# Retention, ELU and maxout layers on one core: the first block from the first chunk of every batch, without a state

## The chip, the cores and the metric

One core of a Trainium2 chip runs the whole program in one launch. The metric is device time in microseconds (us), the median of several executions. TensorE is called PE, VectorE DVE, ScalarE ACT, GpSimd POOL and the engine that issues most DMAs SP.

## The reference

Three layers in a row: a linear attention with a decaying state, a dense layer with an ELU, and a maxout layer.

```python
# q, k, v: (4 batches, 8 heads, 768 steps, 64)
for t in range(S):
    state = gamma[None, :, None, None] * state + np.einsum('bhd,bhe->bhde', k[:, :, t], v[:, :, t])
    y[:, :, t] = scale * np.einsum('bhd,bhde->bhe', q[:, :, t], state)
# x: (3072 tokens, 512)
h = x @ w_in                                    # 512 x 2048
g = np.where(h > 0.0, h, np.exp(np.minimum(h, 0.0)) - 1.0)
x = g @ w_out                                   # 2048 x 512
h = np.maximum(np.maximum(x @ w1, x @ w2), x @ w3)   # 512 x 768 each
return h @ w_out2                               # 768 x 512
```

The state runs through the 768 steps of one batch and starts anew in the next. The matrices w_in to w_out2 are given as 64-bit floats.

## The kernel before

**Attention by chunks.** The 768 steps of a batch are cut into 6 chunks of 128 steps, 24 in all, numbered batch after batch. A chunk needs its own scores (queries times keys, masked by decays), times its values, plus the decayed queries times the state of all earlier chunks; and it hands on state = decay x state + keys times values. Four chunks (CB) make a block of 512 tokens, six blocks in all. Chunks 0 to 3 go through the `wide_` functions, all 128 steps at once; each of them waits for the state of the one before. The later ones go through `scores`, `mask`, `update`, `carry`, `values`, `finish`, in two halves of 64 steps, with `middle` as the state between the halves; `visit(c)` closes chunk c and opens the next. `keys_of` and `queries_of` make the decayed keys (kd) and queries (qd) on POOL. `state` is a pair of tiles that take turns.

**Dense layer by blocks.** For block b and hidden tile f (16 of 128 units), `h1(b, f)` is x @ w_in as 12 products of 512 columns (L400), then the ELU: exp and relu on ACT (L407, L408), max on DVE (L411), the high part gh on ACT (L412) and the low part gl on DVE (L415). `o1(b, f, ...)` adds g @ w_out into four banks of PSUM, again 12 products (L434). Each operand is split into a high and a low half of reduced precision, three products for one. `x2_out` takes the four banks to `x2d` in DRAM.

**Weights.** The 64-bit words of w_in and w_out are loaded in 32 halves of 512 KB (`load_half`, L333; half 2f holds w_in's tile f, 2f + 1 w_out's) and turned into high and low parts: `cv_bits` on ACT (L342), `cv_rest` on DVE (three instructions, L349 to L355), `cv_high` on ACT (L365), `cv_low` on DVE (L370). `cv_rest(n)` also issues half n + 2, since two buffers take turns.

**Order.** All engines run in the order in which the program is written. Until all halves are converted, blocks 0 and 1 go in turns in seven groups of f, so that one new f comes with one or two products that need none. When a group ends its partial sums leave PSUM, and are added to the older ones on DVE (L451); two of the older sums wait in SBUF, the others are stored to `x2d` and loaded again (`renew`):

```python
groups = [(0, 0, 2), (1, 0, 4), (0, 2, 6), (1, 4, 8), (0, 6, 11), (1, 8, KFF), (0, 11, KFF)]
groups += [(b, 0, KFF) for b in range(2, NB)]
seq = [(b, f, f0, f1) for b, f0, f1 in groups for f in range(f0, f1)]
```

In the loop over `seq` step i issues h1 of step i + 1 and then o1 of step i; `third(i)` puts chunks 8 to 12 between them (it opens chunk 8 at i = 23), later blocks carry a chunk at every fourth f. The maxout layer follows from `x2d`. Loads at the start all go through SP's queue: chunk 0, decays, mask, chunks 1 to 3 with halves 0 and 1 between them, chunk 4. A chunk has q and k transposed, by two partition halves of 64 rows, and k and v by token on 128 rows.

Of the kernel before, what the change touches and what calls it, by code (L numbers as in the profile page):

```python
# [42 lines left out]
def kernel(ctx: ExitStack, tc: tile.TileContext, qkv0, qkv, wa, wb, dmask, qdec, cols, out):  # L43
# [33 lines left out]
    def load(c, part=None):  # L77


        if c >= NCHUNK:  # L80
            return

        early = c < EARLY
        src = qkv0 if early else qkv
        if part != 1:
            if c in raw_t:
                return
            if early:
                x = wpool.tile([P, NPAIR, 4, P], F32, tag="w", name="x")
            else:  # L90
                x = ld.tile([P, NPAIR, 4, P], F32, tag="r", name="x")
            raw_t[c] = x
            if early:
                for h, at_, o, n in ((rows(0), 0, 0, 1), (rows(0), 1, 2, 1), (rows(1), 0, 1, 2)):
                    nc.sync.dma_start(
                        out=x[h, :, at_:at_ + n, :].rearrange("d p s t -> d p (s t)"),
                        in_=src[c, :, h, o * P:(o + n) * P].rearrange("p d t -> d p t"),
                    )
            else:
                for g in range(2):  # L100
                    for s in range(2):
                        for p in range(1 if c < 2 * NCH else 2):
                            ps = slice(None) if c < 2 * NCH else slice(p, None, 2)
                            cc = slice((2 * s + (g ^ p)) * P, (2 * s + (g ^ p) + 1) * P)
                            nc.sync.dma_start(
                                out=x[rows(g), ps, s, :], in_=src[c, ps, rows(g), cc].rearrange("p d t -> d p t")
                            )
        if part != 0:
            x = raw_t[c]
            o = 3 * P if early else 4 * P  # L110
            nc.sync.dma_start(
                out=x[:, :, 2:4, :].rearrange("t p s n -> t p (s n)"),
                in_=src[c, :, :, o:].rearrange("p t n -> t p n"),
            )
# [6 lines left out]
    def seat(c, p, r):  # L121
        return r if c < 2 * NCH else r ^ (p & 1)
# [5 lines left out]
    def swap():  # L128
        for g in range(2):
            nc.sync.dma_start(out=qdec_sb[rows(g), 1::2, :], in_=qdec[rows(1 - g), 1::2, :])  # L130
            nc.sync.dma_start(
                out=cols_sb[rows(g), H + 1:H + NPAIR:2], in_=cols[rows(1 - g), H + 1:H + NPAIR:2]
            )

    def later(swapped):
        far = cols_sb[:, H + NPAIR:H + 2 * NPAIR]
        nc.vector.reciprocal(out=far, in_=cols_sb[:, H:H + NPAIR])
        late = qdec_sb[:, 1::2, HC:P] if swapped else qdec_sb[:, :, HC:P]
        by = far[:, 1::2] if swapped else far
        n = NPAIR // 2 if swapped else NPAIR  # L140
        nc.vector.tensor_tensor(out=late, in0=late, in1=by.unsqueeze(2).to_broadcast([P, n, HC]), op=ALU.mult)

    def keys_of(c):
        if c >= NCHUNK:
            return
        kd = at.tile([P, NPAIR, 2, D], F32, tag="kd", name="kd", bufs=2)
        nc.gpsimd.tensor_tensor(  # L147
            out=kd, in0=raw_t[c][:, :, 2, :].rearrange("t p (r d) -> t p r d", r=2),
            in1=cols_sb[:, 0:H].rearrange("t (p r) -> t p r", r=2).unsqueeze(3).to_broadcast([P, NPAIR, 2, D]),
            op=ALU.mult,  # L150
        )
# [22 lines left out]
    def mask(c):  # L174
# [5 lines left out]
        for g in range(2):  # L180
# [3 lines left out]
                in1=d[:, :, g::2, :] if c < 2 * NCH else d[:, :, 0::3, :] if g == 0 else d[:, :, 1:3, :],  # L184
# [5 lines left out]
    def update(c, banks):  # L190
# [3 lines left out]
        kd = st_t[c][1]  # L194
        v = raw_t[c][:, :, 3, :].rearrange("t p (r d) -> t p r d", r=2)
        for p in range(NPAIR):
            for r in range(2):
                for s in range(2):
                    nc.tensor.matmul(  # L199
                        banks[s][rows(seat(c, p, r)), p, :], kd[rows(s), p, r, :], v[rows(s), p, r, :],  # L200
                        start=False, stop=p == NPAIR - 1, skip_group_check=True,
                    )

    def carry(c):
        if c >= NCHUNK:
            return
        new, old, up = state[c % 2], state[1 - c % 2], up_t.pop(c)
        if c % NCH == 0:
            nc.vector.tensor_copy(middle, up[0])
        else:  # L210
            nc.gpsimd.tensor_tensor(
                out=middle, in0=old, in1=cols_sb[:, H:H + NPAIR].unsqueeze(2).to_broadcast([P, NPAIR, D]), op=ALU.mult
            )
            nc.vector.tensor_tensor(out=middle, in0=up[0], in1=middle, op=ALU.add)
        if c % NCH != NCH - 1:
            nc.vector.tensor_tensor(out=new, in0=up[1], in1=middle, op=ALU.add)

    def past(c, cross):
        qd = st_t[c][0]
        for p in range(NPAIR):  # L220
            for g in range(2):
                r, s = seat(c, p, g), g ^ cross
                if c % NCH == 0 and s == 0:
                    continue
                src = middle if s else state[1 - c % 2]
                last = nc.tensor.matmul(  # L226
# [58 lines left out]
    def wide_mix(c):  # L285
        v = raw_t[c][:, :, 3, :].rearrange("t p (r d) -> t p r d", r=2)
        a = a_t.pop(c)
        xo = xo_t[c] = ps_h.tile([P, NPAIR, P], F32, tag="h", name="xo")
        for p in range(NPAIR):
            for r in range(2):  # L290
                nc.tensor.matmul(
                    xo[rows(r), p, :], v[:, p, r, :], a[:, r, p, :],
                    start=p == 0, stop=c == 0 and p == NPAIR - 1,
                )
        if c:
            qd = st_t[c][0]
            for p in range(NPAIR):
                for r in range(2):
                    nc.tensor.matmul(
                        xo[rows(r), p, :], state[1 - c % 2][rows(r), p, :], qd[rows(r), p, :],  # L300
                        start=False, stop=p == NPAIR - 1,
                    )
# [7 lines left out]
    def wide_update(c):  # L310
        kd = st_t.pop(c)[1]
        v = raw_t.pop(c)[:, :, 3, :].rearrange("t p (r d) -> t p r d", r=2)
        up = ps_h.tile([P, NPAIR, D], F32, tag="h", name="up")
        for p in range(NPAIR):
            for r in range(2):
                nc.tensor.matmul(up[rows(r), p, :], kd[:, p, r, :], v[:, p, r, :], start=p == 0, stop=p == NPAIR - 1)
        new, old = state[c % 2], state[1 - c % 2]
        if c == 0:
            nc.vector.tensor_copy(new, up)
        else:  # L320
            nc.vector.tensor_tensor(
                out=new, in0=old, in1=cols_sb[:, H:H + NPAIR].unsqueeze(2).to_broadcast([P, NPAIR, D]), op=ALU.mult
# [866 lines left out]
```

## Time and profile before

| | |
|---|---|
| median of 3 runs | 993.1 us (992.72 to 996.32) |
| the profiled execution | 993.37 us, its span 991.6 us |
| PE busy | 963.9 us, 97% of the span |
| DVE, ACT, POOL busy | 585.1, 343.7, 95.0 us |
| PE's mean granted clock | 0.997 of full speed |
| chain that ended last | PE 83%, DVE 7%, DMA 4%, ACT 3% |

Busy time is of one execution. A line L400 is a line of the kernel above. The chain is followed back from the last instruction to whatever released each step. In a row of time the first number is the start and the second the time covered; PE's products overlap, so their rate is read from one start to the next.

### The profile page before, as it was taken

How to read it: one execution, taken by the hardware profiler on the slowest of the kernel's cores; microseconds unless marked ns; L12 is line 12 of the kernel's file. 1: busy time of each engine (PE TensorE's matmuls, PEld its weight loads, DVE VectorE, ACT ScalarE, POOL GpSimd, SP SyncE). 2: the span in 40 equal slices, each digit the busy share in tenths (PEclk: the TensorE clock that was granted, in tenths of full speed). 3: DMA queues.
4: the chain of work that ended last, by engine and by line, in shares of the span. 5: the costliest groups of instructions: out<-in, count | busy, mean ns of one | idle time of the engine just before them, and what ended most of it. 6: DMA issues, size and time to landing. Idle time of an engine off the chain costs nothing.

```text
span 991.6 us, 16233 instructions
## 1 busy us (share of the span) xinstructions
PE 963.9 (97%) x6644; PEld 785.8 (79%) x6644; DVE 585.1 (59%) x956; ACT 343.7 (35%) x619; POOL 95.0 (10%) x119
## 2 busy tenths in 40 slices
PE   7789999999999999999999999999999999999998
PEld 5667787878888888887888888878888788888886
DVE  2767888753555655666555662477653686436650
ACT  1345554533344444444444553121130212201111
POOL 2310001012111110111110000010100010000100
PEclk9999999999999999999999999999999999999999
DMA  9923345544545555555545444356535556236602
GB/s 225 234 64 105 107 150 185 154 129 113 176 142 160 166 170 165 160 164 168 163 138 170 159 134 164 121 176 204 184 111 202 175 178 199 85 128 208 193 13 85
DMA packets 83721, 151.92 MB, mean 153 GB/s; under 512 B 7232, under 2 KB 58432, under 8 KB 77504
## 3 DMA queue, kind: packets, MB, share of 16 engines
q1 hardware_dynamic: 74000, 94.01, 31.4%
q0 software_dynamic: 7344, 52.69, 16.2%
q10 hardware_dynamic: 2304, 4.20, 1.2%
q8 instruction: 52, 0.85, 0.4%
q14 instruction: 21, 0.17, 0.1%
HBM read 116.53 MB, written 34.34 MB: 152 GB/s over the span
## 4 chain that ended last, share of the span: by engine, by line
PE 83%; DVE 7%; DMA 4%; ACT 3%; issue 1%; POOL 1%; SPq 1%; POOLq 0%; ACTq 0%
PE hp L763 25%; PE acc L434 22%; PE hp L400 22%; PE acc L823 10%; DMA x<-in_qkv 3%; DVE e L411 1%; DVE t L352 1%; PE xs L226 1%; ACT gh L412 1%; PE xs L169 1%; PE xs L239 1%; PE xs L199 1%; DVE w L370 1%; DVE gl L415 1%; DVE t L349 1%
## 5 line engine op out<-in xcount | busy, mean ns | idle before, releaser
L763 PE MATMUL hp<-seat,w 128*128 128x512 f32 x1134 | 259.8, 390 | 3.3 <-DVE m L772 3.3
L763 PEld LDWEIGHTS hp<-seat,w 128*128 128x128 f32 x1134 | 212.1, 188 | 49.7 <-DVE m L772 6.1
L400 PE MATMUL hp<-xh,w 128*128 128x512 f32 x768 | 245.1, 390 | 3.8 <-ACT w L365 2.9
L434 PE MATMUL acc<-gh,w 128*128 128x512 f32 x768 | 205.8, 396 | 4.1 <-ACT gh L412 1.5
L434 PEld LDWEIGHTS acc<-gh,w 128*128 128x128 f32 x768 | 141.8, 188 | 39.1 <-ACT gh L412 3.8
L400 PEld LDWEIGHTS hp<-xh,w 128*128 128x128 f32 x768 | 143.7, 188 | 35.2 <-ACT w L365 4.3
L400 PE MATMUL hp<-xl,w 128*128 128x512 f32 x384 | 141.9, 390 | 0.7 <-DVE xl L261 0.7
L411 DVE SCALAR_TENSOR_TENSOR e<-e,hp 128x512 f32<-128x512 f32 x96 | 65.7, 685 | 124.6 <-ACT e L408 123.7
L434 PE MATMUL acc<-gl,w 128*128 128x512 f32 x384 | 110.7, 390 | 0.0
L407 ACT ACTIVATE e<-hp 128x512 f32<-128x512 f32 x96 | 57.0, 594 | 123.5 <-PE hp L400 121.7
L823 PE MATMUL acc<-w,g 128*128 128x512 f32 x432 | 99.1, 389 | 0.0
L415 DVE TENSOR_TENSOR gl<-e,gh 128x512 fp32r<-128x512 f32 x96 | 66.5, 692 | 52.2 <-ACT gh L412 50.9
L823 PEld LDWEIGHTS acc<-w,g 128*128 128x128 f32 x432 | 81.1, 188 | 16.8
L412 ACT CAST gh<-e 128x512 fp32r<-128x512 f32 x96 | 59.5, 620 | 100.2 <-DVE e L411 100.1
L400 PEld LDWEIGHTS hp<-xl,w 128*128 128x128 f32 x384 | 72.0, 188 | 16.2 <-DVE xl L261 1.0
L434 PEld LDWEIGHTS acc<-gl,w 128*128 128x128 f32 x384 | 72.1, 188 | 15.3
L789 ACT COPY u<-hp 128x512 f32<-128x512 f32 x27 | 15.9, 587 | 143.3 <-PE hp L763 142.4
L657 POOL DMA_DIRECT2D w<-ops_d x48 | 25.6, 533 | 381.8 <-PE hp L763 311.4
L408 ACT ACTIVATE e<-e 128x512 f32<-128x512 f32 x96 | 60.7, 632 | 3.1
L147 POOL TENSOR_TENSOR kd<-x,cols_sb 128x512 f32<-128x512 f32 x24 | 27.4, 1141 | 245.4 <-DMA x<-in_qkv 221.6
L780 ACT CAST g<-e 128x512 fp32r<-128x512 f32 x36 | 22.2, 623 | 51.9 <-DVE e L777 51.5
L772 DVE TENSOR_TENSOR t<-hp,t 128x512 f32<-128x512 f32 x45 | 31.0, 688 | 12.3 <-PE hp L763 12.3
(95 smaller groups left out, 837.2 us busy)
## 6 DMA issues: line engine op xcount, KB each, us to landing
w<-ops_d POOLq DMA_DIRECT2D x48, 1024.0 KB, 5.2
ops_d<-m SPq DMA_DIRECT2D x66, 256.0 KB, 2.8
raw<-in_wa SPq DMA_DIRECT2D x32, 512.0 KB, 3.7
x<-in_qkv SPq DMA_DIRECT2D x24, 512.0 KB, 4.8
raw<-in_wb SPq DMA_DIRECT2D x24, 512.0 KB, 4.4
x<-in_qkv SPq DMA_DIRECT2D x96, 64.0 KB, 2.4
x<-x2d SPq DMA_DIRECT2D x6, 1024.0 KB, 6.7
x<-in_qkv SPq DMA_DIRECT2D x32, 128.0 KB, 4.8
```

What stands on the lines that cost most here:

```text
L147: nc.gpsimd.tensor_tensor(out=kd, in0=raw_t[c][:, :, 2, :].rearrange("t p (r d) -> t p r d", r=2), in1=cols_sb[:, 0:H].rearrange("t (p r) ...
L400: nc.tensor.matmul(hp, w[:, pw, kk * P:(kk + 1) * P], x[px][:, kk, :], start=k == 0, stop=k == len(order) - 1,)
L407: nc.scalar.activation(e, hp, ACTF.Exp)
L408: nc.scalar.activation(e, e, ACTF.Relu, scale=-1.0, bias=1.0)
L411: nc.vector.scalar_tensor_tensor(out=e, in0=e, scalar=-1.0, in1=hp, op0=ALU.mult, op1=ALU.max)
L412: nc.scalar.copy(gh, e)
L415: nc.vector.tensor_tensor(out=gl, in0=e, in1=f32(gh), op=ALU.subtract)
L434: nc.tensor.matmul(acc_t[b][m], w[:, p[0], 512 + m * P:512 + (m + 1) * P], g[p[1]], start=f == f0 and p == first, stop=f == f1 - 1 and p = ...
L657: nc.gpsimd.dma_start(out=ring[n % RING][:, 0:z].rearrange("p s h t -> p (s h t)"), in_=ops_d[:, 4 * k:4 * k + z].rearrange("p s h t -> p ...
L763: nc.tensor.matmul(o, w[:, pw, kk * P:(kk + 1) * P], x[px][:, kk, :], start=first and k == 0, stop=last and k == 5, skip_group_check=True,)
L772: nc.vector.tensor_tensor(out=out, in0=a, in1=c, op=ALU.add)
L823: nc.tensor.matmul(acc, g2[f][:, px, m * P:(m + 1) * P], w[:, pw, :], start=f == 0 and i == 0, stop=f == KF2 - 1 and i == 2, skip_group_ch ...
```

## The change

- A block is now four chunks of the same time, one of each batch: chunk c is batch c % 4, step c // 4 (`place`). Block 0 holds the first chunks of all batches, which have no state before them; `wide_mix` has no state product, and `wide_update` writes `home[c]`, the state of batch c. Later chunks read `home[c % CB]`; a spare tile takes turns with the four. Batches no longer begin within the later chunks, so all of those read a state.
- Chunks 0 to 3 are loaded in pieces, by k, v and the two halves of q and k; ACT's queue issues the second half of chunks 0 to 2 and the mask, POOL's the decays. The keys by token of chunks 0 to 3 come after half 1, halves 2 and 3 between and behind them, then chunk 4, then half 4 and on. The decayed keys overwrite the keys.
- Every second pair of halves up to f = 9 has a buffer of its own, so that halves are issued four ahead.
- Blocks 0 and 1 go in four groups, f = 0 to 4 of block 0 first; each of those five f converts two halves (`lead`). The sums of the second groups are added to `x2d` by a DMA that POOL issues.
- Chunks 4 to 7 are placed between the products of f = 2 to 4. The output rows follow the new token order.

```diff
+    states = const.tile([P, B, NPAIR, D], F32, name="states")
+    def place(c):
+        return c % CB * NCH + c // CB
+    def load(c, part=None, eng=nc.sync):
...
+        for g in range(2):
+            if part not in (None, g):
+                continue
+            for s in range(2):
+                for p in range(1 if wide else 2):
+                    ps = slice(None) if wide else slice(p, None, 2)
+                    o = (2 * s + (g ^ p)) * P
+                    eng.dma_start(out=x[rows(g), ps, s, :], in_=qkv[n, ps, rows(g), o:o + P].rearrange("p d t -> d p t"))
...
     def carry(c):
-        new, old, up = state[c % 2], state[1 - c % 2], up_t.pop(c)
-        if c % NCH == 0:
-            nc.vector.tensor_copy(middle, up[0])
-        else:
...
+        old, new, up = home[c % CB], free_state[0], up_t.pop(c)
...
     def wide_mix(c):
-        if c:
-            qd = st_t[c][0]
...
     def load_half(n):
+            f = n // 2
+            if f % 2 and f < DEEP:
+                if n % 2 == 0:
+                    raws[f] = wpool.tile([P, 2, 512, 2], I32, tag="w", name="raw")
+                r = raws[f][:, n % 2]
...
-        load_half(n + NSTAGE)
+        load_halves(n + 1 + (4 if n + 4 < 2 * DEEP else 2))
...
-    def x2_out(b, f0, f1, keep):
+    def x2_out(b, again=False):
...
-                if f0:
-                    nc.vector.tensor_tensor(out=o[m], in0=acc_t[b][m], in1=o[m], op=ALU.add)
...
+            if again:
+                nc.gpsimd.dma_start(out=to, in_=o, accum_op=ALU.add)
+            else:
+                nc.scalar.dma_start(out=to, in_=o)
...
-    groups = [(0, 0, 2), (1, 0, 4), (0, 2, 6), (1, 4, 8), (0, 6, 11), (1, 8, KFF), (0, 11, KFF)]
+    FA, FB = 5, 9
+    groups = [(0, 0, FA), (1, 0, FB), (0, FA, KFF), (1, FB, KFF)]
...
+    load_decays(nc.gpsimd)
     load(0, 0)
+    load(0, 1, nc.scalar)
+    nc.scalar.dma_start(out=dmask_sb, in_=dmask)
+    load(0, "v")
...
+    load_halves(2)
+    load(0, "k")
+    load(1, "k")
+    load_halves(3)
+    load(2, "k")
+    load(3, "k")
+    load_halves(4)
     load(4)
...
+    def lead(f):
+        def act(_):
+            cv_high(2 * f + 2)
+            cv_bits(2 * f + 3)
+        def vec(_):
+            cv_low(2 * f + 2)
+            cv_rest(2 * f + 3)
+        h1(0, f, (), (), [(cv_low, 2 * f + 1)], [(act, 0)], [(vec, 0)])
+        cv_bits(2 * f + 4)
+        cv_high(2 * f + 3)
+        cv_rest(2 * f + 4)
...
+    lead(0)
+    load(5)
+    wide_update(0)
+    wide_update(1)
...
+    lead(1)
+    load(6)
...
+    o1(0, 0, 0, FA)
+    open_chunk(4)
+    carry(4)
+    keys_of(5)
+    lead(2)
+    load(7)
+    o1(0, 1, 0, FA)
+    visit(4)
+    lead(3)
+    o1(0, 2, 0, FA)
+    visit(5)
+    lead(4)
+    o1(0, 3, 0, FA)
+    visit(6)
+    values(7)
+    o1(0, 4, 0, FA, (0, 1))
+    finish(7)
+    o1(0, 4, 0, FA, (2, 3))
```

Three places show what moves. On PE, from the last scores of block 0 to its first products, the kernel before (xo: values and state products, up: keys times values, hp: h1, xs: the later chunks):

```order
L271 MATMUL sc<-x 128x128 x8
L291 MATMUL xo<-a,x 64x128 x8
L299 MATMUL xo<-qd,state_90 64x128 x8
L316 MATMUL up<-x,kd 64x64 x8
L400 MATMUL hp<-xh,w 128x512 x4
L400 MATMUL hp<-xl,w 128x512 x4
L400 MATMUL hp<-xh,w 128x512 x4
L169 MATMUL xs<-x 64x64 x16
```

and the changed one:

```order
L264 MATMUL sc<-x 128x128 x8
L284 MATMUL xo<-a,x 64x128 x16
L392 MATMUL hp<-xh,w 128x512 x4
L392 MATMUL hp<-xl,w 128x512 x4
L392 MATMUL hp<-xh,w 128x512 x4
L300 MATMUL up<-x 64x64 x16
L392 MATMUL hp<-xh,w 128x512 x4
L392 MATMUL hp<-xl,w 128x512 x4
L392 MATMUL hp<-xh,w 128x512 x4
L300 MATMUL up<-x 64x64 x16
L430 MATMUL acc<-gh,w 128x512 x4
```

The state product L299 is gone, and the states (up) are made behind h1(0, 0) and h1(0, 1), two chunks at a time. On SP's queue of the changed kernel, from half 0 to the loads after half 4 (raw: halves, 64x... rows: q and k, 128x4x128: keys or values by token):

```order
L321 DMA raw<-in_wa 128x1024
L99 DMA x<-in_qkv 64x4x128 x4
L102 DMA x<-in_qkv 128x4x128
L321 DMA raw<-in_wa 128x1024
L102 DMA x<-in_qkv 128x4x128 x2
L321 DMA raw<-in_wa 128x1024
L102 DMA x<-in_qkv 128x4x128 x2
L321 DMA raw<-in_wa 128x1024
L99 DMA x<-in_qkv 64x2x128 x8
L102 DMA x<-in_qkv 128x4x256
L321 DMA raw<-in_wa 128x1024 x5
L99 DMA x<-in_qkv 64x2x128 x8
```

Before, halves 0 to 3 stood behind chunks 2, 3, 4 and 5; now half 4 is the first of the five in a row behind chunk 4, which comes in nine DMAs. On ACT of the changed kernel, from exp of h1(0, 0) to relu of h1(0, 1) (L334: a half's scaling; the ones here are halves 3 and 4):

```order
L399 ACTIVATE e<-hp 128x512
L400 ACTIVATE e<-e 128x512
L357 CAST w<-t 128x512
L334 ACTIVATE t<-raw 128x512
L406 CAST gh<-e 128x512
L334 ACTIVATE t<-raw 128x512
L357 CAST w<-t 128x512
L303 COPY states<-up 128x256 x2
L951 COPY dmask_sb<-dmask_sb 64x8x64
L399 ACTIVATE e<-hp 128x512
L400 ACTIVATE e<-e 128x512
```

The copies of two states and the scalings of two halves now stand between one ELU and the next.

## Rows read from the trace of the kernel before

**Rows 1.** Table by stretches: us, each engine's busy time (instructions), granted clock, DMA share, GB/s.
```profile
10.00:20.00 10.00, 7.01 (x81) 5.81 (x81) 3.93 (x7) 0.59 (x1) 2.30 (x2) 0.83 1.12 267
...
40.00:50.00 10.00, 8.72 (x147) 7.27 (x140) 7.78 (x13) 2.91 (x8) 4.33 (x4) 0.86 1.13 216
...
90.00:100.00 10.00, 10.00 (x45) 8.26 (x44) 7.87 (x14) 6.21 (x11) 0.00 (x0) 1.00 0.29 105
...
200.00:210.00 10.00, 9.47 (x158) 7.61 (x158) 6.10 (x12) 4.73 (x11) 0.75 (x2) 1.00 0.27 77
```

**Rows 2.** The chain that ended last, in order of time: start, length, what.
```profile
24.29 11.65 DMA x<-in_qkv
...
86.57 2.72 PE hp L400 x12
```

**Rows 3.** Instructions in order of time, 0 to 40 us (in brackets idle time, releaser).
```profile
23.48 0.68 ACT L342 ACTIVATE t<-raw 128x512 f32<-128x512 f32 x1 [2.78 <-DMA raw<-in_wa]
...
33.17 1.20 PE L400 MATMUL hp<-xh,w 128*128 128x512 f32 x4
...
36.07 1.39 POOL L147 TENSOR_TENSOR kd<-x,cols_sb 128x512 f32<-128x512 f32 x1 [4.73 <-DMA x<-in_qkv]
```

**Rows 4.** DMA view, 0 to 60 us, in 40 slices; then queue: packets, MB, share.
```profile
GB/s 0 87 180 161 354 347 189 211 309 237 217 241 382 223 217 236 305 236 199 210 260 285 202 200 236 292 276 197 224 221 193 197 264 236 72 208 178 0 0 11
...
q1 hardware_dynamic: 12048, 12.33, 89.5%
```

**Rows 5.** DMA view, 237 to 242 us, where a later chunk is loaded in small pieces.
```profile
q1 hardware_dynamic: 1012, 0.46, 32.2%
```

**Rows 6.** DVE's instructions in order of time, 36 to 84 us.
```profile
41.52 1.27 DVE L349 TENSOR_SCALAR t<-t 128x512 int32<-128x512 int32 x1
...
53.67 0.69 DVE L415 TENSOR_TENSOR gl<-e,gh 128x512 fp32r<-128x512 f32 x1 [0.69 <-ACT gh L412]
54.28 0.68 DVE L370 TENSOR_TENSOR w<-t,w 128x512 fp32r<-128x512 f32 x1
54.88 0.75 DVE L181 TENSOR_TENSOR a<-xs,dmask_sb 128x256 f32<-128x256 f32 x2
55.55 0.75 DVE L261 TENSOR_TENSOR xl<-xs,xh 128x256 fp32r<-128x256 f32 x2
56.21 0.41 DVE L209 COPY dmask_sb<-xs 128x256 f32<-128x256 f32 x1
56.66 0.42 DVE L216 TENSOR_TENSOR state<-xs,dmask_sb 128x256 f32<-128x256 f32 x1
...
72.77 0.42 DVE L349 TENSOR_SCALAR t<-t 128x512 int32<-128x512 int32 x1
...
74.56 0.68 DVE L411 SCALAR_TENSOR_TENSOR e<-e,hp 128x512 f32<-128x512 f32 x1
```

**Rows 7.** Groups by line and form: busy us, mean ns of one | idle before.
```profile
L407 ACT ACTIVATE e<-hp 128x512 f32<-128x512 f32 x96 | 57.0, 594 | 123.5 <-PE hp L400 121.7 <-ACT o L471 0.9 <-DVE t L547 0.9
...
L158 POOL TENSOR_TENSOR qd<-x,qdec_sb 128x512 f32<-128x512 f32 x23 | 30.2, 1314 | 20.7 <-PE xs L226 18.8 <-DVE qdec_sb L141 1.7 <-issue 0.2
...
L211 POOL TENSOR_TENSOR dmask_sb<-state,cols_sb 128x256 f32<-128x256 f32 x17 | 10.9, 639 | 181.7 <-PE xs L226 181.7
```

**Rows 8.** PE's instructions in order of time, 80 to 230 us.
```profile
83.69 1.07 PE L434 MATMUL acc<-gh,w 128*128 128x512 f32 x4
...
193.61 0.69 PE L169 MATMUL xs<-x 64*64 64x64 f32 x32
...
218.33 0.70 PE L434 MATMUL acc<-gh,w 128*128 128x512 f32 x2 [0.75 <-ACT e L407]
```

**Rows 9.** Groups by line and form: the adds of partial sums, and products with states.
```profile
L226 PE MATMUL xs<-qd,dmask_sb 64*64 64x64 f32 x320 | 20.9, 221 | 0.3 <-ACT dmask_sb L249 0.3
...
L226 PE MATMUL xs<-qd,state 64*64 64x64 f32 x272 | 17.8, 222 | 0.1
...
L451 DVE TENSOR_TENSOR part<-acc,part 128x512 f32<-128x512 f32 x12 | 7.4, 682 | 0.0
```

More of the change, by code (lines that the diff above doesn't have):

```diff
@@ L75 @@
     raw_t = {}
-    def load(c, part=None):
-        if c >= NCHUNK:
+    def place(c):
+        return c % CB * NCH + c // CB
+    def load(c, part=None, eng=nc.sync):
+        if c >= NCHUNK or part is None and c in raw_t:
             return
[L83 to L89, printed above, removed]
-            else:
[L91 to L114, printed above, removed]
@@ L229, in past @@
                 )
-        return last
     def value_products(c, banks):
@@ L291, in wide_mix @@
                 nc.tensor.matmul(
-                    xo[rows(r), p, :], v[:, p, r, :], a[:, r, p, :],
-                    start=p == 0, stop=c == 0 and p == NPAIR - 1,
-                )
-        if c:
[L296 to L302, printed above, removed]
+                    xo[rows(r), p, :], v[:, p, r, :], a[:, r, p, :], start=p == 0, stop=p == NPAIR - 1,
+                )
         nc.scalar.copy(x_t[0][0][:, :, c * P:(c + 1) * P], xo)
@@ L315, in wide_update, with load_halves @@
             for r in range(2):
[L316 to L322, printed above, removed]
-            )
-            nc.vector.tensor_tensor(out=new, in0=up, in1=new, op=ALU.add)
+                nc.tensor.matmul(
+                    up[rows(seat(p, r)), p, :], kd[:, p, r, :], v[:, p, r, :], start=p == 0, stop=p == NPAIR - 1
+                )
+        nc.scalar.copy(home[c], up)
     w_t, half = {}, []
     sources = [wa[n // 2][:, n % 2 * 512:(n % 2 + 1) * 512] for n in range(2 * KFF)]
+    raws = {}
+    DEEP = 10
     def load_half(n):
         if n < len(sources):
-            r = stage.tile([P, 512, 2], I32, tag="raw", name="raw")
+            f = n // 2
[4 more added lines that the diff above has]
+            else:
+                r = stage.tile([P, 512, 2], I32, tag="raw", name="raw")
             nc.sync.dma_start(out=r.rearrange("p n w -> p (n w)"), in_=sources[n].bitcast(I32))
             half.append(r)
+    def load_halves(n):
+        while len(half) < min(n, len(sources)):
+            load_half(len(half))
     tmp, keys = {}, [("a", f) for f in range(KFF)]
@@ L390, with h1 @@
     first_use = set()
-    def h1(b, f, then=(), after=(), mid=()):
+    def h1(b, f, then=(), after=(), mid=(), soon=(), next_=()):
         x = x_t[b]
@@ new lines @@
+    wide_mask(0)
+    wide_scores(1)
+    junk(4)
+    wide_mask(1)
+    wide_mix(0)
+    wide_rest(0)
+    wide_scores(2)
+    wide_mask(2)
+    wide_mix(1)
+    cv_bits(0)
+    wide_rest(1)
+    cv_rest(0)
+    cv_high(0)
+    wide_scores(3)
+    wide_mix(2)
+    wide_mask(3)
+    cv_bits(1)
+    cv_low(0)
+    wide_rest(2)
+    wide_mix(3)
+    cv_bits(2)
+    wide_rest(3)
+    cv_rest(1)
+    cv_high(1)
+    cv_rest(2)
+    keys_of(0)
+    load_query_decays(nc.gpsimd)
+    keys_of(1)
+    lead(0)
```

230 lines of the change are left out of this document (93 added, 137 removed).

## Prediction

> **What bounds the kernel now.** I read the table by stretches first, then the chain, then the instructions in order of time. In the table [rows 1] the reader is to see two regimes: from about 90 us on TensorE (PE) is busy 10.00 of 10 us, while in the first 60 us it is not, and the DMA share there is above 1. The chain [rows 2] says what it waits for: loads of x, the last of them 11.65 us long and over at 36 us. After that it is made of blocks of 12 large products, each 2.72 us [rows 2]; whoever shortens another engine there gains nothing. So the change can act at the start, in the small gaps of the conversion stage, and through what it adds to PE.
>
> To compare the two programs I need one place that both pass with the same work behind them. Both run 25 first and 24 second products before chunk 8 is opened. The kernel before has done 10 such products and chunks 4 to 7 when it starts the eleventh at 83.7 us, and opens chunk 8 at 193.6 [rows 8]. In the changed order the same ten products are h1 and o1 of block 0 for f = 0 to 4, with chunks 4 to 7 between them; then comes h1(1, 0). I call the time at which that starts T. Before, its counterpart is 83.7.
>
> **The first products come earlier, but that is not T.** The first block no longer has states: 48 recorded products (L299) and three decayed queries go away, and h1(0, 0) can start when chunk 3 and half 0 have landed; before it starts at 33.2 [rows 3], my estimate for it now is about 25. But what comes next waits for weights. ACT scales half 4 inside lead(0), and behind it in ACT's queue stand the upper half of half 3, two state copies, the mask copy and exp of h1(0, 1); PE's o1(0, 1) and DVE's whole lead(1) hang on those. On SP's queue half 4 stands behind the four first chunks, halves 0 to 3 and all of chunk 4. So **T is the landing of half 4 plus the work of DVE behind it**.
>
> **Landing of half 4.** Ahead of it and with it 8.39 MB move: four chunks and chunk 4 at 1.05 MB each (5.24), five halves at 0.52 (2.62), the mask 0.52. Before, half 0 had landed at 23.5 and chunk 4 at 36.1 [rows 3], with 4.46 and 7.08 MB issued up to them: 0.21 MB per us, and a line that starts at 2.3 us. By that line half 4 lands at 2.3 + 8.39/0.21 = 42.3. The other reading is what has moved: the GB/s row, in slices of 1.5 us [rows 4], sums to 8.2 MB by 36 us, so 8.39 MB by 36.6. Landings lag it since transfers that stand behind already move. Two things of the change bear on it. It takes a chunk in 512-byte pieces everywhere: 2,048 packets for a chunk. A packet in the full queue took 0.895 x 60 x 16 / 12,048 = 71 ns, at 1,023 bytes [rows 4]; in a sparse stretch of pieces of about 455 bytes 25 ns [rows 5]. If a small packet costs half of the 71, nothing changes; if it costs all, the 10,500 packets up to half 4 take 10,500 x 71 / 16 = 46.6 us and it lands at 49. And ACT's queue issues a part of the loads beside SP. I take **39.5**, the middle of the two readings of the same bytes, because the second queue and the shorter list behind half 4 let landings follow closer, and keep 36.6 and 49 for the range.
>
> The Trainium skill, DMA: Bandwidth & Descriptors, section Rules for kernel authors, speaks against the second queue: transfers to the two partition halves serialise ("Don't bother"), and spreading over issuing engines only saves issue time. By it the sum would go by 42.3 in place of 39.5; nothing in this trace has two queues loading halves, so no row decides.
>
> **From there to T, on DVE.** What counts is the distance from one start to the next [rows 6]. One conversion tail, L349 to the next instruction: 72.77 to 74.56, 1.79. A low half (54.28 to 54.88) 0.60, gl (53.67 to 54.28) 0.61; the max of the ELU has the same shape and is taken as 0.60 too. Mask 0.67, remainder 0.66, two halves of the state 2 x 0.45 = 0.90. Behind half 4 stand: its scaling on ACT 0.6; its tail 1.79; four leads of two tails, two lows, max and gl, 4 x 5.98 = 23.9; the later() pair 0.6; four chunks of mask, state and remainder, 4 x 2.24 = 9.0. Together 35.9.
> Waits on that way: (a) in lead(1) ACT does a high half, three copies, exp and relu, four of about 0.6 [rows 7] and two half as wide of 0.4, so 3.2 us, against 2.4 of DVE: 0.8. (b) chunk 4's state waits for qd 1.31 and the decayed state 0.64 on POOL [rows 7], 1.95 less the mask: 1.3. (c) relu of leads 3 and 4: an estimate of 0.5. (d) the last chunk's round PE, ACT, PE, ACT before its remainder: products 0.7, guard 0.3, half of o1 1.36, products 0.5, copies 0.7, with little beside it on DVE: 3.2. (e) a tail beside a POOL instruction: L349 took 1.27 where 0.45 is usual [rows 6]; two such cost 1.6, and I take 1.2. Sum 7.0, so T = 39.5 + 35.9 + 7.0 = 82.4, **1.3 earlier** than 83.7. PE has 3 h1, 5 o1 and about 12 us of small products in these 43 us, less than DVE, so its order does not add.
>
> **From T on.** Before, 83.7 to 193.6 is 109.9 for 39 products of 2.72 (106.1): 3.8 of gaps. The adds of partial sums go from DVE (L451: 12 + 4 + 4 at 0.68, and 4 copies [rows 9]); four group changes stood in that stretch and two stand there now, one of them right at T, each with two copies on ACT and two on DVE. I take 1.3 back, between 0 and 3.8. After 193.6 there are gaps of 0.5 (PE 9.47 of 10 us [rows 1]) and 0.75 [rows 8] in the last of the conversions, beside the reloads and adds of old sums; half of them, **0.6 back**, bounds 0 and 1.3. Added on PE: chunks 6, 12 and 18 now read a state, 48 more records of the kind of 272 against 320 [rows 9]; 32 such take 0.69 [rows 8], so **+1.0**. The eight adding DMAs are issued by POOL, which in the stretches of those group changes has a few instructions like qd and the decayed state [rows 7] to do and x2d is read only before the last stage, so nothing; if the decayed state of chunk 9 came a little later behind four of them, it would still have a whole product pair of cover. The loads of chunks 8 to 11 become nine DMAs instead of five, about 2.6 us more on SP before a half, which is issued two conversions (some 11 us) ahead: nothing; without that cover it would be a gap of 2. Output rows only go elsewhere: same sizes, nothing.
>
> **Sum**: 993.4 (the profiled execution; its span is 991.6, and the median of the runs 993.1) - 1.3 - 1.3 - 0.6 + 1.0 = 991.2.
>
> **Rivals.**
> A, *loads come faster*. For it: the sparse packets of 25 ns [rows 5], slices of up to 382 GB/s [rows 4]; against it: the queue was full and slow for 30 us. At 36.6 it gives 991.2 - 2.9 = 988.3, with somewhat smaller gaps 987; at 0.28 MB per us half 4 lands at 32.3 and the time is 984. Chance 0.31.
> B, *the second queue gives nothing and landings go by 0.21*: 42.3, T 85.2, 994.0. Its place is ACT's wait for half 4; the rule cited above says the same. Chance 0.2.
> C, *slower: small packets*. Each 512-byte packet costs nearly what a 1-KB one did, so ACT stands at half 4 until 47 or later. It decides from 46.4 us (998.1) and ends at 49: 1000.7. For it: 71 ns over many packets that were already 512 bytes; against it: the 25 ns. A fall of PE's granted clock (0.83 and 0.86 in stretches with idle PE [rows 1]) would push the same way, since h1 precedes exp in each lead. Chance 0.15.
>
> **Chances.** The forecast, half 4 between 36.4 and 41: 0.34. About 0.5% (5 us) is what a measurement can tell from no change. Faster by more is A, 0.31; within it are the forecast and B, 0.54; slower is C, 0.15. The range takes A to 984 and C to 1000; about 0.15 lies outside. The likeliest side's own range is 988 to 998.
>
> **What would show it.** Right: ACT idle before its sixth scaling of a weight half (half 4) until 38 to 41 us, with DMA as the releaser; DVE over 85% busy from there to T; T near 82; PE 10.00 in the stretches behind it, with no DVE releaser at group changes. Wrong: half 4 landed by 35 or after 45; DVE idle between leads because PE or POOL is late; gaps at the first waits for x2d on its way out, which would mean that the new copies, not the old adds, hold the banks.

## The result, and the profile after

| | before | after |
|---|---|---|
| median of 6 runs each, one chip | 995.84 us (992.72 to 998.15) | 1001.8 us (999.28 to 1003.38) |
| the profiled execution, its span | 993.37, 991.6 us | 1000.9, 999.1 us |
| PE's mean granted clock | 0.997 | 0.99 |

The ratio of the times is 1.0063, with a 95% interval of 1.0039 to 1.0087: slower by 0.6%, where 991.2 us and no measurable change were forecast, and outside the range of 984 to 1000.

The prediction cut the time at T, the start of h1(1,0), and at the opening of chunk 8. The same cuts in the changed kernel (the start of half 4's scaling on ACT, the first row below the table, stands for its landing; the first rows of T and of chunk 8 follow it):

| stretch, us | forecast | after | difference |
|---|---|---|---|
| start to half 4's scaling | 39.5 | 38.50 | -1.0 |
| from there to T | 42.9 | 52.35 | +9.45 |
| T to chunk 8 (109.9 before) | 108.6 | 111.51 | +2.9 |
| chunk 8 to the end of the span (798.0 before) | 798.4 | 796.74 | -1.7 |

```profile
38.50 0.66 ACT L334 ACTIVATE t<-raw 128x512 f32<-128x512 f32 x1 [3.96 <-DMA raw<-in_wa]
```
```profile
90.85 0.39 PE L392 MATMUL hp<-xh,w 128*128 128x512 f32 x1
...
202.36 0.69 PE L165 MATMUL xs<-x 64*64 64x64 f32 x32
```

So the loss is in the second row. The table by stretches (columns as in [rows 1]: us, PE, PEld, DVE, ACT, POOL with instructions, granted clock, DMA share, GB/s) shows it:

```profile
40.00:50.00 10.00, 8.48 (x109) 6.89 (x110) 8.16 (x16) 6.09 (x13) 1.72 (x2) 1.00 0.65 188
50.00:60.00 10.00, 6.25 (x140) 4.96 (x139) 9.62 (x19) 4.36 (x10) 3.02 (x4) 0.90 0.83 217
60.00:70.00 10.00, 9.63 (x150) 7.60 (x148) 4.74 (x9) 4.30 (x10) 1.15 (x2) 0.76 0.71 208
70.00:80.00 10.00, 7.81 (x76) 6.20 (x80) 5.90 (x13) 3.89 (x8) 3.27 (x3) 0.83 0.51 180
80.00:90.00 10.00, 7.02 (x163) 5.50 (x154) 5.68 (x13) 2.10 (x10) 2.37 (x2) 0.83 0.20 56
90.00:100.00 10.00, 8.99 (x40) 7.10 (x39) 4.46 (x8) 3.81 (x8) 0.00 (x0) 1.00 0.17 61
```

From 60 to 90 us DVE works 4.7 to 5.9 of 10 us; over all of the second row it is busy for 35.55 of 52.35 us, 68%, where over 85% was forecast. PE's granted clock is 0.76 to 0.83 there, which at the two levels of 2.4 and 1.2 GHz means parts at the lower one. From 60 to 70 us PE is busy for 9.63 of 10 us, in part at the lower level; from 70 to 90 us neither engine is full, and the two wait for each other. The chain that ended last, 58 to 66 us (start, length, what), and PE's rows at the three places where it repeats (in brackets the idle time before, and who ended it):

```profile
57.51 0.66 DVE a L177 x2
58.17 0.34 DVE xl L254
58.56 5.50 PE hp L392 x12
64.08 0.61 ACT e L399
64.71 0.64 ACT e L400
65.38 0.69 DVE e L403
```
```profile
58.56 2.07 PE L392 MATMUL hp<-xh,w 128*128 128x512 f32 x4 [1.07 <-DVE xl L254]
...
72.19 2.07 PE L392 MATMUL hp<-xh,w 128*128 128x512 f32 x4 [2.45 <-DVE xl L254]
...
84.68 1.17 PE L230 MATMUL xs<-a,x 64*64 64x64 f32 x29 [2.45 <-DVE xl L254]
...
90.85 0.39 PE L392 MATMUL hp<-xh,w 128*128 128x512 f32 x1
```

Why h1 waits for xl (L254, the remainder of a chunk's output), of which it reads nothing: the PSUM pool `ps_h` has four banks that go round. h1's hp takes one, `values(c)` two and `open_chunk(c + 1)` two; so hp of h1(0, f + 1) gets the first bank of `values(c)`, and that is free when DVE has made xl from it. No run gave h1 a bank of its own; that it waits for the bank is read from the order of the pool and from the releaser in the rows above. And this is where xl stands in DVE's queue (lines of the changed kernel: L403 is the max, L411 gl, L341 the first instruction of a tail, L177 the mask):

```profile
42.18 0.69 DVE L403 SCALAR_TENSOR_TENSOR e<-e,hp 128x512 f32<-128x512 f32 x1 [0.50 <-ACT e L400]
...
50.17 0.42 DVE L208 TENSOR_TENSOR dmask_sb<-xs,dmask_sb 128x256 f32<-128x256 f32 x1 [1.31 <-POOL dmask_sb L205]
...
65.38 0.69 DVE L403 SCALAR_TENSOR_TENSOR e<-e,hp 128x512 f32<-128x512 f32 x1 [5.15 <-ACT e L400]
...
66.58 0.42 DVE L341 TENSOR_SCALAR t<-t 128x512 int32<-128x512 int32 x1
...
68.38 0.68 DVE L411 TENSOR_TENSOR gl<-e,gh 128x512 fp32r<-128x512 f32 x1
68.98 0.42 DVE L341 TENSOR_SCALAR t<-t 128x512 int32<-128x512 int32 x1
...
71.06 0.74 DVE L177 TENSOR_TENSOR a<-xs,dmask_sb 128x256 f32<-128x256 f32 x2
71.73 0.74 DVE L254 TENSOR_TENSOR xl<-xs,xh 128x256 fp32r<-128x256 f32 x2
...
77.86 0.69 DVE L403 SCALAR_TENSOR_TENSOR e<-e,hp 128x512 f32<-128x512 f32 x1 [4.00 <-ACT e L400]
...
89.93 0.76 DVE L254 TENSOR_TENSOR xl<-xs,xh 128x256 fp32r<-128x256 f32 x2 [4.18 <-ACT xh L251]
```

Between the max of one lead (65.38) and xl (71.73) lie two conversion tails, gl and the mask. So a lead is a ring: h1, exp, relu, max, two tails, xl, and only then the next h1, with DVE idle 4 to 5 us while PE and ACT have their turn. Leads came every 13.63 and 12.49 us (58.56, 72.19, 84.68). The 13.63 are 5.52 of h1 at the lower clock (granted 0.50), 1.30 of exp and relu, 6.35 from max to xl and 0.46 from there to the next h1. In the kernel before, at the visit of [rows 6], no tail stood between max and xl, and xl came 3.25 us behind this max:

```profile
52.30 0.69 DVE L411 SCALAR_TENSOR_TENSOR e<-e,hp 128x512 f32<-128x512 f32 x1 [0.51 <-ACT dmask_sb L249]
```

DVE's idle times behind half 4 that are rowed with a releaser are 0.50, 1.31, 5.15, 4.00 and 4.18 = 15.1 us, against 5.8 of waits without contention in the prediction's list (a) to (d); that is the 9.3. One term holds most of it: the two waits for relu, 5.15 and 4.00, are the prediction's (c), "relu of leads 3 and 4: an estimate of 0.5". The others came near, (a) 0.50 for 0.8, (b) 1.31 for 1.3, (d) 4.18 for 3.2.

### The profile page after: what moved, and what is told of

Read it like the earlier page. It is cut to its first block, busy times and chain, and to the rows that moved or that the text cites. A ratio compares the mean times of both kernels' runs of the same rounds, so it can differ in the third digit from the quotient of the medians.

```text
span 999.1 us, 16295 instructions
## 1 busy us (share of the span) xinstructions
PE 964.7 (97%) x6648; PEld 785.1 (79%) x6648; DVE 573.4 (57%) x931; ACT 347.4 (35%) x630; POOL 104.9 (10%) x134
## 4 chain that ended last, share of the span: by engine, by line
PE 82%; DVE 6%; DMA 4%; ACT 3%; issue 3%; POOL 1%; SPq 0%; ACTq 0%; POOLq 0%; DVEq 0%
PE hp L745 25%; PE acc L430 22%; PE hp L392 22%; PE acc L805 10%; DMA x<-in_qkv 2%; DVE e L403 1%; PE xs L230 1%; DVE t L344 1%; PE xs L165 1%; PE xs L218 1%; DMA ops_d<-m 1%; ACT gh L406 1%; DVE gl L411 1%; ACT e L400 1%; PE xs L194 1%
## 5 line engine op out<-in xcount | busy, mean ns | idle before, releaser
L392 PE MATMUL hp<-xh,w 128*128 128x512 f32 x768 | 248.5, 395 | 8.8 <-DVE xl L254 3.5
L392 PEld LDWEIGHTS hp<-xh,w 128*128 128x128 f32 x768 | 145.8, 191 | 40.1 <-DVE xl L254 3.8
L403 DVE SCALAR_TENSOR_TENSOR e<-e,hp 128x512 f32<-128x512 f32 x96 | 65.7, 685 | 148.9 <-ACT e L400 148.6
L411 DVE TENSOR_TENSOR gl<-e,gh 128x512 fp32r<-128x512 f32 x96 | 68.9, 717 | 48.8 <-ACT gh L406 47.4
L144 POOL TENSOR_TENSOR x<-x,cols_sb 128x512 f32<-128x512 f32 x24 | 27.6, 1152 | 223.1 <-DMA x<-in_qkv 208.6
L754 DVE TENSOR_TENSOR t<-hp,t 128x512 f32<-128x512 f32 x45 | 31.0, 688 | 12.3 <-PE hp L745 12.3
```

The source lines that it names most:

```text
L144: nc.gpsimd.tensor_tensor(out=kd, in0=kd, in1=cols_sb[:, 0:H].rearrange("t (p r) -> t p r", r=2).unsqueeze(3).to_broadcast([P, NPAIR, 2, D ...
L392: nc.tensor.matmul(hp, w[:, pw, kk * P:(kk + 1) * P], x[px][:, kk, :], start=k == 0, stop=k == len(order) - 1,)
L403: nc.vector.scalar_tensor_tensor(out=e, in0=e, scalar=-1.0, in1=hp, op0=ALU.mult, op1=ALU.max)
L411: nc.vector.tensor_tensor(out=gl, in0=e, in1=f32(gh), op=ALU.subtract)
L754: nc.vector.tensor_tensor(out=out, in0=a, in1=c, op=ALU.add)
```

## The experiments

Stage A is the start of h1(0, 2) to T, stage B is T to the opening of chunk 8. The start of h1(0, 2) itself varied from 45.7 to 49.1 us over all runs, though only three of them changed anything ahead of it, so the stages tell more than the time. Each row of the table is one profiled execution; only e8, e10 and e11 were timed more often, 12 times each, with the changed kernel 6 times beside them. The changed kernel had A 44.62 and 43.95, B 111.51 and 111.74 in its two profiles.

| run, what it edits | A | B | span |
|---|---|---|---|
| e1: DVE's second tail behind the visit | 37.03 | 111.22 | 992.3 |
| e13: ACT's scaling behind the visit | 46.05 | 111.57 | 1000.9 |
| e6: both | 35.03 | 111.41 | 989.6 |
| e2: on PE, o1 behind the visit | 44.76 | 110.79 | 998.5 |
| e3: visit ahead of o1 and both tails | 38.38 | 111.80 | 994.9 |
| e4, e12: products of zeros in PE's waits | 42.93, 41.34 | 110.75, 111.24 | 999.4, 996.9 |
| e5: half 4 ahead of chunk 4 | 43.31 | 111.00 | 996.7 |
| e9: loads on one queue | 45.32 | 111.35 | 999.7 |
| e7: e6, e5, copies of sums earlier | 38.34 | 110.05 | 990.3 |
| e8: e6, copies of sums earlier | 35.83 | 109.49 | 990.2 |
| e10: e8 with zeros | 36.25 | 109.17 | 989.4 |
| e11: e8, gl and low halves on POOL | 37.93 | 110.04 | 992.4 |

**DVE's order alone** (e1).

```diff
-        cv_rest(2 * f + 4)
+        if f < 2:
+            cv_rest(2 * f + 4)
...
     visit(4)
+    cv_rest(8)
     lead(3)
```

> T is the start of the first product of the second batch block, h1(1,0): 90.85 us in the changed kernel. Bank theory: h1(0,f+1) waits on a PSUM bank that VectorE's remainder xl frees, and xl stands behind two conversion tails; with the second tail of leads 2 to 4 put behind the visit, xl comes as soon as ScalarE has copied xh, which in the changed kernel's profile was 1.3 us before it at 70.4 and at 82.9, and not before it at 58.1. T comes 2 to 3 us earlier (88 to 89), VectorE's waits for relu shrink, and the time falls by as much. VectorE theory (the work of VectorE alone sets T, as the prediction had it): the work is the same, only in another order, T and the time stay within 0.5 us.

A fell by 7, more than twice the 2 to 3 expected for T (T itself came 5.9 us earlier, at 84.92), with the same work on every engine. PE's rows of this run, and one of the second profile of the changed kernel:

```profile
59.02 1.97 PE L392 MATMUL hp<-xh,w 128*128 128x512 f32 x4 [0.98 <-DVE xl L254]
...
70.29 1.19 PE L392 MATMUL hp<-xh,w 128*128 128x512 f32 x4 [0.98 <-DVE xl L254]
...
79.98 1.02 PE L230 MATMUL xs<-a,x 64*64 64x64 f32 x32 [0.98 <-DVE xl L254]
```
```profile
73.96 1.19 PE L392 MATMUL hp<-xh,w 128*128 128x512 f32 x4 [2.45 <-DVE xl L254]
```

At the first place the wait for xl is nearly what it was, 0.98 and 1.07: there ACT began xh, which xl reads, only at 57.56 in the changed kernel, half a us ahead of xl. At the other two it is 1.5 us shorter. The first four products of h1(0, 4) take 1.19 instead of 2.07, but that is not shown to come from the shorter wait: in the second profile of the changed kernel they took 1.19 too, behind the old wait of 2.45. Over all of A the granted clock was 0.95, against 0.85 and 0.88 in the changed kernel. The idea that DVE's work alone sets T is ruled out.

**The whole visit earlier** (e3). It comes ahead of both tails on DVE, and ahead of o1(0, f - 1) on PE.

```diff
-    def lead(f):
+    def lead(f, c=None):
...
             cv_low(2 * f + 2)
+            if c is not None:
+                visit(c)
             cv_rest(2 * f + 3)
...
-    lead(2)
+    lead(2, 4)
     load(7)
     o1(0, 1, 0, FA)
-    visit(4)
```

> The chunk's visit goes ahead of o1(0,f-1) on TensorE and ahead of the two conversion tails and gl on VectorE. Bank theory: the bank is free about 8 us after the start of h1(0,f), while o1 still runs; the leads come every 9 to 10 us instead of 13.6 and 12.5, T is 79 to 84 and the time falls by 7 to 11 us, below the kernel before. VectorE theory: same work, T stays at 90 to 91 and the time within 1 us of the changed kernel's.

h1(0, 3) and h1(0, 4) came 9.8 us apart (62.77, 72.59) as expected, but the first of them 14.0 us after h1(0, 2): the visit stood there for chunk 4's state (1.23 us), and later visits for DVE's max (1.12 and 1.70), whose bank is the next in the round for them. A 38.4, T 87.2: later than expected and no better than e1.

**The clock** (e4, then e12). `awake(k)` adds k products of zeros to o1's accumulator, which needs no bank:

```diff
+    def awake(k):
+        for i in range(k):
+            nc.tensor.matmul(acc_t[0][i % KDM], zeros[:, 0:P], zeros, start=False, stop=False, skip_group_check=True)
...
         open_chunk(c + 1)
+        awake(k[0])
         finish(c)
+        awake(k[1])
```

> Products of zeros are added to o1's accumulator in the idle places of TensorE between 52 and 85 us; no order and no wait is changed otherwise. Clock theory: the products h1(0,3), h1(0,4) and o1(0,4) took 5.28, 4.17 and about 4 us instead of 2.72 because the granted clock had fallen to 1.2 GHz in the wait before them; kept up, these take 2.7 to 3.0, T comes 4 to 5.5 us earlier (85.5 to 87) while VectorE's remainder xl still precedes each h1. Bank theory alone (the waits themselves are the loss and the clock's fall is hidden in them): T stays at 90 to 91. If the products of zeros delay what stands behind them, T is later by up to 2 us.

> The changed kernel with its orders as they are, and 5, 10 and 10 products of zeros only in TensorE's last wait of each visit, that for xl (the run with more of them had put 8 ahead of the cross products, and so delayed xl itself). h1(0,2) to T is 44.6 us in the changed kernel. If the fall of the clock in these waits is the larger part of the loss, 39 to 41; if the wait for xl is, with the clock's fall as a part of some 2 us on top, 42 to 43.5; if the clock costs nothing, 44 to 45.

In e4 eight zeros stood ahead of the first cross products (decayed queries with the state between the halves, L218), which xl needs, and h1(0, 3) came 15.8 us after h1(0, 2), where the changed kernel took 12.3; so its A tells only a part. In e12 A is 2.6 to 3.3 us shorter, between the two ranges expected. Its rows:

```profile
60.67 2.27 PE L392 MATMUL hp<-xh,w 128*128 128x512 f32 x4
...
72.94 1.20 PE L392 MATMUL hp<-xh,w 128*128 128x512 f32 x4 [0.18 <-DVE xl L254]
...
84.11 0.96 PE L230 MATMUL xs<-a,x 64*64 64x64 f32 x29 [0.19 <-DVE xl L254]
```

At h1(0, 3) the clock had already fallen in the waits before, but rose sooner: the twelve products took 3.96 us, 5.28 and 5.11 in the two profiles of the changed kernel. From the third row to T the granted clock was 1.00 and the time 4.65 us, against 0.72 and 6.17 and 6.19 (e5 had 1.00 and 4.66 there without zeros, so a single run does not prove what the zeros did; what the clock costs is read either way). Over all of A it was 0.96 in e12, 0.88 in e5, 0.85 and 0.88 in the changed kernel, and 0.95 in e6 and e8. The orders give back 8.9 us in all (44.3, the mean of the two profiles, to 35.4, the mean of e6 and e8). So about 3 of that go with the clock alone, and 5.9, from e12's 41.34 to 35.4 at nearly the same clock, are the shorter waits themselves. In its section "A second HAM failure mode: psum-queue depth-cycling" the Trainium skill, TensorE: Matmul & The Clock Gate, tells of small idles between groups of products that go round PSUM banks, and of a clock that falls and rises with them; this trace agrees, with 2.07 against 1.20 us for four products.

**Which queue matters** (e2, e13, e6). The edits of e2 (PE alone) and e13 (ACT alone), for each lead alike; e6 is that of e13 with e1's.

```diff
-    o1(0, 1, 0, FA)
     visit(4)
+    o1(0, 1, 0, FA)
     lead(3)
```
```diff
-        cv_high(2 * f + 3)
+        if f < 2:
+            cv_high(2 * f + 3)
...
     visit(4)
+    cv_high(7)
     lead(3)
```

> On TensorE alone, o1(0,f-1) goes behind the chunk's visit instead of ahead of it; VectorE's and ScalarE's orders stay as in the changed kernel. Bank theory: xl still stands behind both conversion tails, so h1(0,f+1) waits as long; but o1 now runs in that wait, TensorE is not idle ahead of h1 and the granted clock stays up, so a lead takes 11.3 us instead of 13.6 and 12.5 and h1(0,2) to T 40 to 42.5 us instead of 44.6. If the order of TensorE alone were the cause, the stage would take 37 us, as with VectorE's order changed; if neither clock nor order matter, 44 to 45.

> Only ScalarE's scaling of the lead's second half goes behind the visit; VectorE's second tail stays ahead of mask and xl. If VectorE's queue holds the bank, xl comes no earlier though the guard copies do: h1(0,2) to T 43 to 45 us (44.6 in the changed kernel, 37.0 with the tail alone moved, 35.0 with both). If the guard copies on ScalarE were what held the visit, 37 to 41.

> As the kernel with the tail behind the visit, and ScalarE's scaling w of the lead's second half goes behind the visit too. Stage measured: from the start of h1(0,2) to T, the start of h1(1,0): 44.6 us in the changed kernel, 37.0 with the tail behind the visit. There ScalarE's guard copies still stood behind that scaling, which waits for VectorE's first tail, and TensorE waited for them 1.83, 0.57 and 0.54 us. If the chain over the bank still sets the pace, the stage takes 34 to 36 us; if VectorE's work sets it by now, 36.5 to 37.5.

e2 missed (A 44.76): o1 did run in the wait, but another wait, of 2.41, 1.88 and 1.88 us for ACT's guard copies (one column of each bank of `values`, L240, ahead of the cross products), came ahead of it. Behind the second of these o1 ran at the lower clock, 0.51 of full speed for 5.21 us, and h1 behind it at the upper one:

```profile
68.87 0.36 PE L218 MATMUL xs<-qd,dmask_sb 64*64 64x64 f32 x1 [1.88 <-ACT cols_sb L240]
...
69.50 2.07 PE L430 MATMUL acc<-gh,w 128*128 128x512 f32 x4
...
74.71 1.09 PE L392 MATMUL hp<-xh,w 128*128 128x512 f32 x4
```

e13 alone is 1.4 to 2.1 us worse, and 1 above what was expected: the guard came earlier, xl did not, and PE waited longer in one piece.

```profile
73.02 2.07 PE L392 MATMUL hp<-xh,w 128*128 128x512 f32 x4 [4.17 <-DVE xl L254]
```

Behind e1's edit the same move gains 2.0 (35.03), because then xl waits for ACT. There DVE is busy again, as the prediction had it: from half 4's scaling (39.36) to T (82.12) it takes 42.8 us, and DVE works for 36.0 of them. The slice before T:

```profile
70.00:80.00 10.00, 8.84 (x200) 7.22 (x198) 9.59 (x19) 5.04 (x13) 1.96 (x3) 1.00 0.40 140
```

**The loads** (e9, e5). The edits of e9 and of e5 (`cv_rest(0)` issues half 4):

```diff
-    load(0, 1, nc.scalar)
+    load(0, 1, nc.sync)
...
-        load(c, 1, nc.scalar)
+        load(c, 1, nc.sync)
```
```diff
     load_halves(4)
-    load(4)
...
     cv_rest(0)
+    load(4)
```

> The changed kernel with the second halves of queries and keys of chunks 0 to 2 issued by SP, not by ScalarE. Theory that a second issuing queue brings the loads in earlier: the first h1 starts 1.5 to 4 us later (25.3 to 30.7 us in the runs so far), and half 4's scaling at 42 or later instead of 38.5 to 40.6. Theory that the transfers share what bounds them anyway: both within the spread of the runs so far. The loss of the changed kernel does not come from there in either case.

> The load of chunk 4 is issued behind the load of weight half 4 instead of ahead of it. Half 4 was issued at 33.04 us though its buffer was free at about 28, and landed at 38.5; now it is issued at about 28 and lands at 33 to 35, and ScalarE's wait of 3.96 us goes. Theory that the loads set the start of the stage: T comes 2 to 3.5 us earlier. Theory that the leads' round of TensorE, ScalarE and VectorE behind chunk 4's state sets it: the idle time moves to the wait for chunk 4 (landed 36.07, now 38 to 40), and T stays within 1 us or comes up to 2 us later.

With one queue the first h1 starts at 25.39 (25.30 with two) and half 4 is scaled at 38.12 (38.50): of the 1.5 to 4 us that a second queue was to bring nothing shows, as far as one run in a spread of 25.3 to 30.7 can tell. That is what the Trainium skill's DMA: Bandwidth & Descriptors, Rules for kernel authors, says; but half 4 did not land at 42.3 without it, so the price that rival B hung on the rule was wrong. In e5 half 4's scaling no longer waited, and T came at 90.42, nearly as late as without that edit (90.85). That fits the theory that the round behind chunk 4 sets it; but the first h1 started at 28.74 in this run, 3.4 us later than in the changed kernel's profile, so it does not exclude a gain from the earlier load.

**The copies of the first sums, and a version of all that helped** (e7, e8).

```diff
+    x2_out(0)
     h1(1, 0, [(cv_low, n)], [(cv_high, n + 1)])
-    x2_out(0)
```

> As the kernel before it in this call, and two more orders, each read in its own stretch. The load of chunk 4 goes behind weight half 4: half 4's scaling is no longer waited for, and h1(0,2) starts at 46 to 47 as in the run that had that alone (47.1), against 46.2 to 48.8 without it: little or no gain. The copies of the first partial sums go ahead of h1(1,0)'s exp on ScalarE: o1(1,0) waited 1.01 us for them and o1(1,1) 0.46 us for gh, behind them; if these copies cost the stretch from T to the opening of chunk 8 its surplus, that stretch falls from 111.5 us to 110 to 110.5 (109.9 in the kernel before). All together: the time is 2 to 5 us below the kernel before.

> The conversion tail and ScalarE's scaling behind the visit, and the copies of the first partial sums ahead of h1(1,0)'s exp. From the stages of the runs that had them: h1(0,2) to T 35 to 36 us (44.6 in the changed kernel) and T to chunk 8 110.0 (111.5), so 9 to 11 us below the changed kernel on the same chip and 1 to 4 us below the kernel before. If the bank wait were not the cause, within 1 us of the changed kernel.

In the changed kernel ACT took the first copy of the sums only behind exp, relu and gh of h1(1, 0), and PE stood at the next block's first product for it:

```profile
97.46 0.72 PE L430 MATMUL acc<-gh,w 128*128 128x512 f32 x2 [1.01 <-ACT o L450]
...
103.67 2.11 PE L430 MATMUL acc<-gh,w 128*128 128x512 f32 x8 [0.46 <-ACT gh L406]
```

With the copies ahead these waits are gone and B is 110.05 and 109.49. A is 38.34 in e7 against 35.03 in e6, and e5's load order is all that differs in it, so e8 leaves that out. The changed kernel was run on e8's chip too:

> The changed kernel as it is, for its time on the same chip as the three below and for the spread of its stages: h1(0,2) to T 44 to 46 us, T to the opening of chunk 8 111 to 112, time 0.4 to 0.9% above the kernel before.

There it had 1000.21 us, 1.0081 of the kernel before (1.0057 to 1.0106); e8 has 992.54, a ratio of **1.0005 (0.9985 to 1.0026)**. Order alone takes back the loss: e8 is 7.7 us below the changed kernel there, somewhat less than the 9 to 11 expected. The 1 to 4 us below the kernel before that I expected did not show.

**Further, without a gain** (e10, e11). Both start from e8. e10 has e4's `awake` with k = (1, 5), (0, 4) and (0, 4) in the three visits; e11 has this:

```diff
-        nc.vector.tensor_tensor(out=gl, in0=e, in1=f32(gh), op=ALU.subtract)
+        (nc.gpsimd if b == 0 and 2 <= f < FA else nc.vector).tensor_tensor(out=gl, in0=e, in1=f32(gh), op=ALU.subtract)
...
+        def low(n):
+            cv_low(n, nc.gpsimd if f >= 2 else nc.vector)
...
-        h1(0, f, (), (), [(cv_low, 2 * f + 1)], [(act, 0)], [(vec, 0)])
+        h1(0, f, (), (), [(low, 2 * f + 1)], [(act, 0)], [(vec, 0)])
```

> As the kernel with two orders, with one to five short products of zeros in TensorE's wait for xl in each visit (0.23 us each at the high clock). Clock theory: h1(0,3) no longer opens at 1.2 GHz (its first four products took 2.08 us instead of 1.20), T 1 to 2 us earlier than without them. If VectorE's work sets T by now, within 0.5 us; if the zeros stand in the way of h1, up to 1 us later.

> As the kernel with two orders, with gl and the second low half of leads 2 to 4 computed by GpSimd instead of VectorE: 6 instructions of 0.60 us off VectorE, 6 of about 1.1 us on GpSimd. If VectorE's work sets the pace of these leads after the reordering, T comes 2 to 3.6 us earlier; if the round over TensorE and ScalarE does, within 0.5 us; if GpSimd's work slows VectorE's beside it (as 1.2 to 1.6 us instead of 0.68 in single instructions so far), or holds up the queries of the next chunk behind it on GpSimd, 0.5 to 3 us later.

e10 is at 1.0008 (0.9989 to 1.0027), no different from e8; its zeros did not keep the clock up at h1(0, 3) either, whose first four products took 2.27 us by their row, so it does not decide what that would be worth. e11 is slower than e8, 1.0037 (1.0017 to 1.0058), by 2.0 us in the medians of 12 executions each. Its DVE and POOL rows at one place:

```profile
68.78 1.80 DVE L344 SCALAR_TENSOR_TENSOR t<-raw,t 128x512 int32<-128x512 int32 x1
```
```profile
68.76 1.27 POOL L411 TENSOR_TENSOR gl<-e,gh 128x512 fp32r<-128x512 f32 x1 [2.77 <-ACT gh L406]
```

An instruction of 0.69 us takes 1.80 where the moved one starts with it. In A eight instructions of DVE run longer than usual (0.68 to 1.80 us) and cost 6.2 us together, five of them (1.49 to 1.80) 4.8; e8 has three (1.10 to 1.52) that cost 2.1. So some 4 us come back, more than the 3.6 that left DVE, and three of the five stand in the tail ahead of an xl. How this adds up to the 2.1 by which A is longer than in e8 was not traced further. The Trainium skill, Perfetto Trace Analysis, section Optimizing Scalar/DVE Operations, says of moving work between these two that it "might not help", since they share an SBUF read port; the run agrees.

## Why the prediction was wrong

- **The first products, and half 4: right.** h1(0, 0) started at 25.30 (about 25), half 4 was scaled at 38.50 after ACT had waited 3.96 us for its load (39.5; "idle until 38 to 41"). It is ACT's fifth scaling, not the sixth. Rivals A and C fall with it; B's 42.3 too, though one run came within 1 us of it. C had the direction, and its 1000.7 lies near the measured time, but by luck: its small packets did not hold half 4. Over the runs in which it waited for the load it came at 38.1 to 41.3, 39.8 on average; that 39.5, the middle of two readings, is so near has no reason that a run shows, and is luck.
- **DVE's work of 35.9: right.** From half 4's scaling to T there are 52.35 us, of which 15.1 are DVE's waits; 37.2 remain with the scaling, against 35.9 and the 1.2 of (e) for tails beside POOL.
- **"PE has 3 h1, 5 o1 and about 12 us of small products in these 43 us, less than DVE, so its order does not add": the step that failed.** A sum of work was taken for a bound, though h1's bank is held by xl behind DVE's own tails, so that PE's and ACT's turns add to DVE's. In the sum this is (c), relu of leads 3 and 4, an estimate of 0.5 without a working: it measured 9.15. The waits (a) to (d) were found by following data; none followed the bank. They measured 15.1 together, not 5.8. With the tail and ACT's scaling moved, the same stretch takes 42.8 (e6) and 43.6 (e8), near the forecast's 42.9: and in e6 DVE's waits are 5.3 us, near the 5.8: the sum would have held for that order.
- **The clock** was named inside rival C as pushing the same way, without a price. With it up for most of the stretch A was 2.6 to 3.3 us shorter (e12). It fell in the ring and its waits, with half 4 on time, so not by C's small packets.
- **T to chunk 8: wrong by 2.9.** 1.3 was to come back; the adds did go, but the copies behind gh took their place, as "the new copies, not the old adds, hold the banks" had allowed. With the copies moved, B is 109.2 to 110.05, level with the 109.9 before, so the 1.3 did not come even then.
- **From chunk 8 on: not separable.** 796.74 against 798.4; over the runs this stretch went from 795.3 to 798.3 without a change in it, as much as the +1.0 and -0.6 in question. That the DMAs on POOL cost nothing holds at the first group change behind chunk 8's opening: PE 10.00 of 10 us at 200 to 220.
- **Why e8 is not faster than the kernel before, either, stays open.** In its profile half 4 was scaled at 41.32, 2.8 us later than in that of the changed kernel, and T was 84.90, against 83.7 before; had it come at 38.50, T would be near 82 by the same distance, an estimate. But the one profile of the kernel before was not taken beside e8, and its span of 991.6 us is longer than the 990.2 of e8's, so the two do not explain the equal times. How much the kernel before varies at its start, and what makes the loads vary, was not tried.

## What to carry to other kernels

Before saying that an engine's order does not add, go round the pool: for each tile of a shared set of banks name the tile it replaces, the instruction that frees that one, and what stands ahead of this instruction in its queue. A reader that frees a bank belongs ahead of work that nobody waits for; here moving three instructions per lead behind it was worth 7 us, with no work saved. And test an order on all queues of the ring: PE's alone gave nothing, ACT's alone made it worse, and ACT's behind DVE's gave 2 us more.

## What the hardware showed that I had not expected

After waits of 1.91, 0.77 and 1.07 us between small products the granted clock was at its lower level, 0.50 from 58.56 to 63.84: the twelve products there took 5.3 us instead of the 2.72 of [rows 2]. The same wait of 2.45 us ahead of h1(0, 4) left the clock at 0.66 over its twelve products in one profile of the changed kernel and at 1.00 in the other. The first block's start by loads varied by over 5 us (25.3 to 30.7) in kernels whose programs do not differ up to there. And an elementwise DVE instruction took 2.6 times its usual 0.69 us when a POOL instruction started beside it.
